# One attention and two expert layers on one core: a PSUM bank for every fourth block of the first layer, lows on another engine, and three small products put further back

## The chip, the cores and the metric

The program runs on one core of one Trainium2 chip. The metric is the device time of one execution in microseconds (us). Three executions of the kernel before took 758.89, 758.95 and 762.05 us; the median is 758.95 us. A fourth execution was recorded by the hardware profiler.

The engines are named as in the profile: PE is TensorE (PEld its weight loads), DVE is VectorE, ACT is ScalarE, POOL is GpSimd, SP is SyncE, which here only issues DMAs. Each engine runs its own instructions in their order, and waits for others by semaphores.

## The reference

Three stages, each the input of the next (4 x 768 = 3072 tokens, 384 columns):

```python
# attention, per batch and head; f = sigmoid(f_logit)
state = f[:, :, t, :, None] * state + einsum('bhd,bhe->bhde', k[:, :, t], v[:, :, t])
y[:, :, t] = einsum('bhd,bhde->bhe', q[:, :, t], state)
# first layer: 384 -> 2048 -> 384
h = x @ w_in;  x = np.maximum(0.01 * h, h) @ w_out
# second layer: 8 experts (384 -> 1024 -> 384), 384 tokens each
logits = x @ w_gate
# all (token, expert) pairs in falling order of their logit: a token goes to the first expert that has room
for e in range(E):
    out[assigned == e] = np.maximum(x[assigned == e] @ w1[e], 0.0) @ w2[e]
```

## The kernel before

**Numbers.** PE multiplies 16-bit numbers. Where more accuracy is wanted, a value is kept as a 16-bit high part and a 16-bit rest, its low part, and a product is made of three: high by high, high by low, low by high. A 128 x 384 block of the first layer's hidden values (tile `hp`, one PSUM bank) is so the sum of nine matmuls of 384 columns.

**First layer.** The 24 attention tiles of 128 tokens form eight groups of three, `gi` = 0 to 7. `first(gi)` makes the 16 blocks `f` of a group's hidden values: nine matmuls into `hp`, then ACT copies it scaled by 0.01, DVE takes the larger of the two (both tile `g`, in SBUF), and for each pair of blocks ACT makes the high part `gh` and DVE the low part `gl`. A bank of `hp` is free when DVE's `g` has read it. `second(gi, n, m)` multiplies `gh` and `gl` by `w_out` into `xp`, three times per group. The order is first(0), first(1), second(0), first(2), second(1), and so on to first(6); first(7) has the router's `logits` of the groups 5 and 6 among its blocks (tile `lp`), and the second halves of the groups 5, 6 and 7 come after it.

**PSUM.** There are eight banks. The pool `psum` has three of them under the tag `mm`, which `hp` and `xp` (later also the experts' `hp` and `yp`) take in turn. The pool `banks[0]` has five under the tag `at`, which the attention's products take in turn: `P`, two `A`, `kT`, `y`, `U` for a tile, and the early gate products `pg`. For first(7) that pool is closed and another, `banks2`, takes its five banks: three for the router (tag `rt`, `lp` among them) and two for turned tokens.

**What sets the order.** A driver runs first and second as the main stream and attention, the weights' preparation and later the router and the token lists as side streams: each yields the number of nanoseconds of main-stream matmuls after which it is taken up again. The tile framework's scheduler then orders each engine's instructions by its own estimates, save those given to `keep_in_program_order`. Beside the first layer, ACT and DVE also split the experts' weights (`xw_s` is loaded, ACT makes `xw_h`, DVE `xw_l`, SP stores both).

**Second layer.** `route()` finds in seven rounds which tokens each expert gets. A round has levels of three small products with DVE between them (`ge` by `oh` into `c`, then `cnt`, then `tot`) and ends in `slots_of`, which counts places by two products with `ones` and `tri` into `ps`. `token_list` turns places into a list of token numbers by the products `pi` (with `ohs` and `rh`) and `pj`; POOL then fetches the tokens by indirect DMAs (`xg`), SP turns them by DMA (`x2T`). `expert(r)` makes eight `hp` blocks of nine matmuls, ACT writes the high part `hh`; the low part `hl` is made by DVE for odd `f`, and for even `f` of experts 0 to 5 by POOL from a second copy that ACT writes (tile `g` in the profile). Then three `yp` of 24 matmuls each go out through POOL's scatter. The seventh round's lists are those of experts 6 and 7 (`E - 2` and `E - 1`).

Every instruction shows as line 85, the recording helper, so the profile is read by tile names.

Of the kernel before, what the change touches and what calls it, by code (L numbers as in the profile page):

```python
# [9 lines left out]
F32 = mybir.dt.float32  # L10
# [82 lines left out]
def body(tc, qk, v, f_logit, w_in, w_out, w_gate, w1, w2, out):  # L93
# [8 lines left out]
    E = w_gate.shape[1]  # L102
# [4 lines left out]
    GW = 384  # L107
# [5 lines left out]
    with ExitStack() as ctx:  # L113
# [4 lines left out]
        psum = ctx.enter_context(tc.tile_pool(name="psum", bufs=1, space=bass.MemoryType.PSUM))  # L118
        ctxL, ctxR, ctxP = (ctx.enter_context(ExitStack()) for _ in range(3))
        banks = [ctxP.enter_context(tc.tile_pool(name="banks", bufs=1, space=bass.MemoryType.PSUM, reuse_waits="tile"))]  # L120
# [9 lines left out]
        def mm(o, l, r, start, stop):  # L130
            return PE.matmul(o, l, r, start=start, stop=stop, skip_group_check=True)
# [405 lines left out]
        def first(gi, nn, gx):  # L537
            xh, xl = gx[:, :KT], gx[:, KT:]
            N = 128 * nn
            gp = g2pool[0] if gi == LAST else gpool  # L540
            gh = gp.tile([128, NF, GW], F16, name="gh")
            gl = gp.tile([128, NF, GW], F16, name="gl")
            gh_[gi], gl_[gi] = gh, gl
            for f in range(NF):
                while ("in", f * NPC // NF) not in ready:
                    yield None
                fs = slice(128 * f, 128 * (f + 1))
                hp = psum.tile([128, GW], F32, name="hp", tag="mm", bufs=3)[:, :N]
                for c in range(KT):
                    mm(hp, winh[:, c, fs], xh[:, c, :N], c == 0, False)  # L550
                    yield N / 2.4
                    mm(hp, winh[:, c, fs], xl[:, c, :N], False, False)
                    yield N / 2.4
                    mm(hp, winl[:, c, fs], xh[:, c, :N], False, c == KT - 1)
                    if c < KT - 1:
                        yield N / 2.4
                a = SG / (SX * SWI)
                with tc.high_priority():
                    if f % 2 == 0:
                        g = work.tile([128, 2, GW], F32, name="g32")  # L560
                    t = g[:, f % 2, :N]
                    i = copy(t, hp, 0.01 * a)
                    fed.append((i, DVE.scalar_tensor_tensor(t, hp, a, t, op0=OP.mult, op1=OP.max)))
                    big[0] += 3 * KT
                    if f % 2:
                        s = slice(f - 1, f + 1)
                        copy(gh[:, s, :N], g[:, :, :N])
                if f % 2 == 0 and f:
                    tc.keep_in_program_order(low())
                if f % 2:  # L570
                    def low(s=s, g=g):
                        return DVE.tensor_tensor(gl[:, s, :N], g[:, :, :N], gh[:, s, :N], op=OP.subtract)
                yield N / 2.4
            low()
# [50 lines left out]
        R = {}  # L625
# [92 lines left out]
        def route():  # L718
# [6 lines left out]
            for rnd in range(E - 1):  # L725
# [73 lines left out]
                x48 = small([128, 2, NT], "x48", BF16)  # L799
# [16 lines left out]
                s1 = slots_of(x48, 2)  # L816
# [17 lines left out]
            x48 = small([128, 2, NT], "x48", BF16)  # L834
            for i in range(2):
                DVE.tensor_scalar(x48[:, i, :], asg, last[i], None, op0=OP.is_equal)
            yield 500.0
            s1 = slots_of(x48, 2)
            DVE.tensor_scalar(s1[:, 1, :], s1[:, 1, :], -float(NT * 128 // E), 0.0, op0=OP.add, op1=OP.max)
            for i in range(2):  # L840
                lists.append((E - 2 + i, s1[:, i, :]))
# [7 lines left out]
        GAP = (1700.0, 700.0, 550.0, 2000.0, 3400.0)  # L849
        lists = []  # L850

        def slots_of(x, n):

            w = n * NT
            xf = x.rearrange("p a b -> p (a b)")
            ps = bank([128, 2, 2 * NT], "ps")
            mm(ps[:, 1, :w], R["ones"], xf[:, :w], True, True)
            mm(ps[:, 0, :w], R["tri"], xf[:, :w], True, True)
            tot = small([128, 2 * NT], "totc")
            DVE.tensor_copy(tot[:, :w], ps[:, 1, :w])  # L860
            inc = small([128, 2 * NT], "inc")
            DVE.tensor_tensor_scan(inc[:, :w], R["ones"][:, :w], tot[:, :w], 1.0, op0=OP.mult, op1=OP.add)
            DVE.tensor_tensor(inc[:, :w], inc[:, :w], tot[:, :w], op=OP.subtract)
            s = small([128, 2, NT], "s1")
            sf = s.rearrange("p a b -> p (a b)")
            DVE.tensor_tensor(sf[:, :w], ps[:, 0, :w], inc[:, :w], op=OP.add)
            DVE.tensor_tensor(sf[:, :w], sf[:, :w], xf[:, :w], op=OP.mult)
            return s

        def token_list(r, s):  # L870

            si = small([128, NT], "si", I32)
            DVE.tensor_scalar(si, s, -1.0, None, op0=OP.add)
            lo = small([128, NT], "lo", I32)
            DVE.tensor_scalar(lo, si, 31, None, op0=OP.bitwise_and)
            hi = small([128, NT], "hi", I32)
            DVE.tensor_scalar(hi, si, 5, None, op0=OP.arith_shift_right)
            lob = small([128, NT], "lob", BF16)
            DVE.tensor_scalar(lob, lo, 1.0, None, op0=OP.add)
            hib = small([128, NT], "hib", BF16)  # L880
            DVE.tensor_copy(hib, hi)
            yield 2500.0 if r else 600.0

            G = 4
            one = rw.tile([128, NT // G, 32, G], BF16, name="ohs", bufs=1)
            for h in range(2):
                x = slice(NT // G // 2 * h, NT // G // 2 * (h + 1))
                lg4 = lob.rearrange("p (a g) -> p a g", g=G)[:, x, None, :].to_broadcast([128, NT // G // 2, 32, G])
                DVE.tensor_tensor(one[:, x], lg4, R["thr5"][:, x], op=OP.is_equal)
                yield 300.0  # L890
            h12 = small([128, 12, NT], "h12", BF16)
            DVE.tensor_tensor(h12, hib[:, None, :].to_broadcast([128, 12, NT]), R["i12"], op=OP.is_equal)
            rh = small([128, 2, 12, NT], "rh", BF16)
            DVE.tensor_tensor(rh[:, 0], h12, R["jn"], op=OP.mult)
            DVE.tensor_scalar(rh[:, 1], h12, pcol, None, op0=OP.mult)
            yield 1800.0
            pi = bank([128, 24, G], "pi")
            for a in range(NT // G):
                mm(pi, one[:, a], rh[:, :, :, a * G:(a + 1) * G].rearrange("p v h g -> p (v h) g"),
                   a == 0, a == NT // G - 1)  # L900
            pm = small([128, 24, G], "pm", F16)
            DVE.tensor_tensor(pm, pi, R["d15"][:, None, :].to_broadcast([128, 24, G]), op=OP.mult)
            pd = small([128, 24], "pd", F16)
            with nc.allow_low_precision("one whole number and zeros"):
                DVE.tensor_reduce(pd, pm, axis=AX.X, op=OP.add)
            yield 1200.0
            pj = bank([128, 6, 4], "pj")
            mm(pj, R["join"], pd, True, True)
            pq = small([128, 6, 4], "pq")
            DVE.tensor_tensor(pq, pj, R["quarter"][:, None, :].to_broadcast([128, 6, 4]), op=OP.mult)  # L910
            ti = small([128, 2, 3], "ti")
            DVE.tensor_reduce(ti.rearrange("p a b -> p (a b)"), pq, axis=AX.X, op=OP.add)
            idx = rw.tile([128, 3], I32, name="idx", bufs=E)
            DVE.scalar_tensor_tensor(idx, ti[:, 0, :], 128.0, ti[:, 1, :], op0=OP.mult, op1=OP.add)

            row = rw.tile([128, 3], I32, name="row", bufs=E)
            if r:
                DVE.tensor_scalar(row, idx, 1.0, None, op0=OP.add)
            else:
                f = small([128, 3], "f3")  # L920
                DVE.tensor_scalar(f, idx, 1.0, None, op0=OP.add)
                DVE.scalar_tensor_tensor(row, f, float(NT * 128 - 128), f, op0=OP.is_le, op1=OP.mult)
                DVE.tensor_scalar(R["place"], R["i384"], s[:, NT - 1:NT], None, op0=OP.is_equal)
            LISTS["x", r] = row, idx
# [69 lines left out]
        def expert(r):  # L994
# [20 lines left out]
            for f in range(NF1):  # L1015
# [8 lines left out]
                        yield N / 2.4  # L1024
                with tc.high_priority():
                    ACT.activation(hh[:, f, :], hp, AF.Relu, bias=0.0, scale=1.0)
                    if f % 2 == 0 and r < E - 2:
                        t = work.tile([128, 2 * GW], F32, name="g32")[:, :N]
                        ACT.activation(t, hp, AF.Relu, bias=0.0, scale=1.0)
                        POOL.tensor_tensor(hl[:, f, :], t, hh[:, f, :], op=OP.subtract)  # L1030
                    else:
                        DVE.scalar_tensor_tensor(hl[:, f, :], hp, 0.0, hh[:, f, :], op0=OP.max, op1=OP.subtract)
# [295 lines left out]
```

## Time and profile before

| | us |
|---|---|
| median of the three runs | 758.95 |
| the profiled execution | 760.42 |
| its span, first to last instruction | 758.6 |
| PE busy with matmuls | 722.8 |
| DVE busy | 548.5 |
| ACT busy | 339.8 |
| POOL busy | 94.4 |

The span and the engines' busy times are of the profiled execution; 1.8 us of its 760.42 lie outside the span. Busy times overlap. A matmul of 384 columns is recorded as 0.33 us long while the next one starts 0.16 us after it, so time that PE loses is read from start to start.

### The profile page before, as it was taken

To read this page: it belongs to the slowest core of one execution; us is meant where nothing else is said; L and a number is where in the kernel's file an instruction comes from. 1 tells how busy PE (TensorE), PEld (TensorE's weight loads), DVE (VectorE), ACT (ScalarE), POOL (GpSimd) and SP (SyncE) were. 2 spreads that over 40 slices of the span, in tenths; PEclk is the share of its full clock that TensorE was granted. 3 is DMA by queue.
4 is the path that set the end of the run, shared out by engine and by line. 5 is a ranking of instruction groups with operands and counts; after the bars stand their busy time and mean duration, and the time that the engine had idled before them with its cause. 6 is when DMAs were issued, how large, how long until landed. Compare 5 with 4: busy or idle time off the path is not lost.

```text
span 758.6 us, 15366 instructions
## 1 busy us (share of the span) xinstructions
PE 722.8 (95%) x5871; PEld 472.8 (62%) x5871; DVE 548.5 (72%) x1607; ACT 339.8 (45%) x708; POOL 94.4 (12%) x124
## 2 busy tenths in 40 slices
PE   8997899999999999999999999999999999999995
PEld 6774666677676577566666666555555555556663
DVE  7999999998857867876964858687686776873220
ACT  7677555567736755754753652000123123222220
POOL 3000000000000000000000001010244534535111
PEclk9999999999999999999999999999999999999998
DMA  9997554799896898998899300050396566677500
GB/s 230 208 251 200 156 143 133 198 294 253 232 268 180 238 262 203 265 272 223 218 269 244 131 2 2 23 197 22 109 266 168 167 196 159 230 193 212 149 31 32
DMA packets 116444, 137.09 MB, mean 181 GB/s; under 512 B 67729, under 2 KB 99474, under 8 KB 114322
## 3 DMA queue, kind: packets, MB, share of 16 engines
q1 hardware_dynamic: 110994, 101.50, 52.0%
q0 software_dynamic: 5376, 34.61, 13.5%
q8 instruction: 46, 0.75, 0.4%
q14 instruction: 28, 0.23, 0.1%
HBM read 86.52 MB, written 34.60 MB: 160 GB/s over the span
## 4 chain that ended last, share of the span: by engine, by line
PE 50%; DVE 21%; DMA 11%; issue 10%; ACT 3%; POOL 3%; SPq 1%; POOLq 0%; ACTq 0%; DVEq 0%
PE hp L85 19%; PE xp L85 17%; PE yp L85 4%; DMA fT<-in_f_logit 4%; PE y L85 3%; DVE g L85 3%; DVE woutu L85 2%; DVE gl L85 2%; DMA xw_s<-in_moe_w 2%; DMA win_e<-in_moe_w_in 1%; PE A L85 1%; PE c L85 1%; PE P L85 1%; POOL out L85 1%; DVE am L85 1%
## 5 line engine op out<-in xcount | busy, mean ns | idle before, releaser
L85 PE MATMUL hp<-xT,winh 128*128 128x384 f16 x768 | 190.7, 328 | 10.0 <-ACT winh L85 4.9
L85 PE MATMUL xp<-wo,gh 128*128 128x384 f16 x768 | 191.1, 326 | 2.8 <-DVE g L85 1.8
L85 PE MATMUL hp<-xT,winl 128*128 128x384 f16 x384 | 125.6, 328 | 0.5 <-DVE winl L85 0.4
L85 PE MATMUL xp<-wo,gl 128*128 128x384 f16 x384 | 125.0, 326 | 0.0
L85 PEld LDWEIGHTS <-gh 128*128 128x128 f16 x912 | 83.9, 97 | 45.7 <-issue 3.2
L85 PEld LDWEIGHTS <-winh 128*128 128x128 f16 x768 | 73.2, 98 | 53.8 <-issue 7.2
L85 PE MATMUL hp<-x2T,w1e 128*128 128x384 f16 x576 | 98.9, 326 | 0.4 <-ACT x2T L85 0.3
L85 PE MATMUL yp<-w2e,hh 128*128 128x384 f16 x384 | 94.4, 326 | 0.0
L85 DVE SCALAR_TENSOR_TENSOR g<-hp,g 128x384 f32<-128x384 f32 x128 | 70.2, 554 | 28.1 <-ACT g L85 27.7
L85 ACT ACTIVATE g<-hp 128x384 f32<-128x384 f32 x152 | 72.0, 484 | 37.1 <-PE hp L85 26.5
L85 PEld LDWEIGHTS <-w1e 128*128 128x128 f16 x576 | 52.4, 97 | 32.8 <-issue 0.7
L85 ACT ACTIVATE gh<-g 128x768 f16<-128x768 f32 x64 | 53.9, 842 | 29.0 <-DVE g L85 28.9
L85 PEld LDWEIGHTS <-gl 128*128 128x128 f16 x528 | 48.9, 97 | 28.5 <-DVE gl L85 0.5
L85 ACT ACTIVATE xw_h<-xw_s 128x768 f16<-128x768 f32 x64 | 53.1, 839 | 29.0 <-DMA xw_s<-in_moe_w 23.9
L85 PE MATMUL yp<-w2e,hl 128*128 128x384 f16 x192 | 62.5, 326 | 0.0
L85 DVE TENSOR_TENSOR gl<-g,gh 128x768 f16<-128x768 f32 x64 | 60.9, 952 | 2.0 <-ACT gh L85 2.0
L85 DVE SCALAR_TENSOR_TENSOR xw_l<-xw_s,xw_h 128x768 f16<-128x768 f32 x64 | 60.2, 951 | 1.7 <-ACT xw_h L85 1.5
L85 ACT ACTIVATE hh<-hp 128x384 f16<-128x384 f32 x64 | 31.4, 490 | 59.7 <-PE hp L85 53.7
L85 POOL IOTA jp<- 128x128 f32 x2 | 0.5, 237 | 455.8 <-PE hp L85 455.7
L85 ACT ACTIVATE x<-yp 128x384 f32<-128x384 f32 x24 | 11.8, 490 | 91.1 <-PE yp L85 76.4
L85 PEld LDWEIGHTS <-winl 128*128 128x128 f16 x384 | 37.6, 98 | 24.0 <-DVE winl L85 1.7
L85 DVE SCALAR_TENSOR_TENSOR hl<-hp,hh 128x384 f16<-128x384 f32 x40 | 22.2, 555 | 41.2 <-ACT hh L85 41.0
(262 smaller groups left out, 1123.9 us busy)
## 6 DMA issues: line engine op xcount, KB each, us to landing
xw_s<-in_moe_w SPq DMA_DIRECT2D x64, 384.0 KB, 4.2
qkT<-in_qk SPq DMA_DIRECT2D x48, 192.0 KB, 5.1
wout_s<-in_moe_w_out SPq DMA_DIRECT2D x16, 384.0 KB, 3.3
w1d<-xw_h SPq DMA_DIRECT2D x32, 192.0 KB, 4.1
w1d<-xw_l SPq DMA_DIRECT2D x32, 192.0 KB, 4.2
w2d<-xw_h SPq DMA_DIRECT2D x32, 192.0 KB, 3.6
w2d<-xw_l SPq DMA_DIRECT2D x32, 192.0 KB, 4.4
fT<-in_f_logit SPq DMA_DIRECT2D x24, 192.0 KB, 3.9
```

The costliest lines, as they stand in the source:

```text
L85: i = f(*args, **kwargs)
```

## The change

Four edits. In `first`, the blocks `f` = 3, 7, 11 and 15 of the groups 2 to 6 take their bank from the attention's five instead of `mm`'s three. In `expert`, the low parts of even blocks of expert 0 are made by DVE, as odd ones are, and no longer by ACT and POOL. After the last round, the stream yields 3100 instead of 500 before the last `slots_of`, and the first of its two products is kept in program order. For expert 6, `token_list` yields 1500 instead of 1800 before `pi`.

```diff
@@ first
-                hp = psum.tile([128, GW], F32, name="hp", tag="mm", bufs=3)[:, :N]
+                if f % 4 == 3 and 2 <= gi < LAST:
+                    hp = banks[0].tile([128, GW], F32, name="hp", tag="at", bufs=5)[:, :N]
+                else:
+                    hp = psum.tile([128, GW], F32, name="hp", tag="mm", bufs=3)[:, :N]
@@ route, after the last round
-            yield 500.0
-            s1 = slots_of(x48, 2)
+            yield 3100.0
+            s1 = slots_of(x48, 2, tc.keep_in_program_order)
@@ slots_of
-        def slots_of(x, n):
+        def slots_of(x, n, put=lambda i: None):
...
-            mm(ps[:, 1, :w], R["ones"], xf[:, :w], True, True)
+            put(mm(ps[:, 1, :w], R["ones"], xf[:, :w], True, True))
@@ token_list
-            yield 1800.0
+            yield 1500.0 if r == E - 2 else 1800.0
@@ expert
-                    if f % 2 == 0 and r < E - 2:
+                    if f % 2 == 0 and 0 < r < E - 2:
```

What the scheduler makes of it is more than the diff tells. On PE, the order up to the last group is the same, and only the banks differ. At the start of first(7), where `hp` is that group's first block and `lp` are the router's logits, the order before was:

```order
L85 LDWEIGHTS winh
L85 MATMUL hp<-xT,winh 128x384
L85 LDWEIGHTS gh
L85 MATMUL lp<-wgc,gh 128x16
L85 LDWEIGHTS gl
L85 MATMUL lp<-wgc,gl 128x8
L85 LDWEIGHTS winh
L85 MATMUL hp<-xT,winh 128x384
```

and now is (rows from the block's eighth matmul on):

```order
L85 LDWEIGHTS winh
L85 MATMUL hp<-xT,winh 128x384
L85 LDWEIGHTS winl
L85 MATMUL hp<-xT,winl 128x384
L85 LDWEIGHTS gh
L85 MATMUL lp<-wgc,gh 128x16
L85 LDWEIGHTS gl
L85 MATMUL lp<-wgc,gl 128x8
L85 LDWEIGHTS gh
L85 MATMUL lp<-wgc,gh 128x16
```

The logits begin behind all nine matmuls of the block instead of behind its first, and the first 18 of them follow each other. The second logits tile takes the bank that the last block of group 6 had.

On DVE, in expert 0, between the first round's slots and the next round's `ge` (which PE's product `c` waits for; `key`, `di` and `v` are steps of the router, `hl` the low parts), the order was:

```order
L85 TENSOR_TENSOR eq_7646<-lg,m 128x192
L85 SCALAR_TENSOR_TENSOR hl<-hp,hh 128x384
L85 TENSOR_TENSOR s_7632<-ps,inc 128x48
L85 TENSOR_SCALAR key<-m 128x24
L85 TENSOR_TENSOR eq_7646<-eq_7646,wdt 128x192
L85 TENSOR_TENSOR s_7632<-s_7632,x_7594 128x48
```

and now is:

```order
L85 TENSOR_SCALAR wi<-mx,p_6230 128x1
L85 SCALAR_TENSOR_TENSOR hl<-hp,hh 128x384
L85 SCALAR_TENSOR_TENSOR inc<-ones,totc 128x48
L85 TENSOR_REDUCE m<-lg 128x24
L85 TENSOR_TENSOR inc<-inc,totc 128x48
L85 TENSOR_TENSOR eq_7640<-lg,m 128x192
L85 TENSOR_TENSOR s_7626<-ps,inc 128x48
L85 TENSOR_SCALAR key<-m 128x24
L85 TENSOR_TENSOR eq_7640<-eq_7640,wdt 128x192
L85 SCALAR_TENSOR_TENSOR hl<-hp,hh 128x384
L85 TENSOR_TENSOR s_7626<-s_7626,x_7590 128x48
```

All eight low parts of expert 0 now stand in DVE's order ahead of that `ge`; four did before. From the last level of round 0 (its `tot`) to the `ge` there are five instead of three. On PE the product `c` behind this `ge` stands six matmuls of 384 columns later than before. In expert 5, the last `ps` stands four such matmuls later, and `pi` and `pj` of experts 6 and 7 stand 14 later.

On POOL, while expert 5 runs (`hl` its low parts, `xg` the tokens of expert 6, `w1e` the weights of expert 7), the order was:

```order
L85 DMA out<-x_9653,idx 3072x384
L85 TENSOR_TENSOR hl<-g_9718,hh 128x384
L85 DMA xg<-x2d,row 128x768 x3
L85 TENSOR_TENSOR hl<-g_9774,hh 128x384
L85 TENSOR_TENSOR hl<-g_9819,hh 128x384
L85 DMA w1e<-w1d,wi 128x6144
```

and now is:

```order
L85 DMA out<-x_9623,idx 3072x384
L85 TENSOR_TENSOR hl<-g_9699,hh 128x384
L85 DMA xg<-x2d,row 128x768
L85 TENSOR_TENSOR hl<-g_9766,hh 128x384
L85 DMA xg<-x2d,row 128x768 x2
L85 TENSOR_TENSOR hl<-g_9795,hh 128x384
L85 DMA w1e<-w1d,wi 128x6144
```

One low part now stands between the first and the second fetch.

## Rows read from the trace of the kernel before

**Rows 1.** The page, part 1: busy time, share of the span, instructions

```profile
PE 722.8 (95%) x5871; PEld 472.8 (62%) x5871; DVE 548.5 (72%) x1607; ACT 339.8 (45%) x708; POOL 94.4 (12%) x124
```

**Rows 2.** Waits of PE, 180 to 470: us in total, times, longest us

```profile
PE hp L85 <- DVE g L85: 3.2, 5, 1.6
PE xp L85 <- DVE g L85: 1.8, 1, 1.8
```

**Rows 3.** Waits of PE, 230 to 260, in first(4)

```profile
PE hp L85 <- DVE g L85: 2.6, 3, 1.6
```

**Rows 4.** Timeline of PE, first(4): start, length, instruction, [idle before <-releaser]

```profile
248.68 0.49 PE L85 MATMUL hp<-xT,winh 128*128 128x384 f16 x2 [1.62 <-DVE g L85]
...
251.60 0.49 PE L85 MATMUL hp<-xT,winh 128*128 128x384 f16 x2
```

**Rows 5.** Timeline of ACT, first(4)

```profile
246.81 0.84 ACT L85 ACTIVATE xw_h<-xw_s 128x768 f16<-128x768 f32 x1 [2.02 <-DMA xw_s<-in_moe_w]
```

**Rows 6.** Timeline of DVE, first(4)

```profile
248.06 0.56 DVE L85 SCALAR_TENSOR_TENSOR g<-hp,g 128x384 f32<-128x384 f32 x1 [1.82 <-ACT g L85]
...
249.40 0.55 DVE L85 SCALAR_TENSOR_TENSOR g<-hp,g 128x384 f32<-128x384 f32 x1
```

**Rows 7.** Timeline of ACT behind the wait of `xp`

```profile
197.03 0.84 ACT L85 ACTIVATE xw_h<-xw_s 128x768 f16<-128x768 f32 x1 [0.97 <-DMA xw_s<-in_moe_w]
197.78 0.58 ACT L85 ACTIVATE kp<-kT 128x512 f32<-128x512 f32 x1
```

**Rows 8.** Timeline of PE there

```profile
199.06 0.95 PE L85 MATMUL U<-ld_v,kp 128*112 128x96 f32 x8
```

**Rows 9.** Timeline of PE, the first matmul of first(7)

```profile
433.90 0.33 PE L85 MATMUL hp<-xT,winh 128*128 128x384 f16 x1
```

**Rows 10.** Timeline of DVE, the last block of group 6

```profile
435.79 0.55 DVE L85 SCALAR_TENSOR_TENSOR g<-hp,g 128x384 f32<-128x384 f32 x1
```

**Rows 11.** Timeline of PE, expert 0

```profile
561.22 0.33 PE L85 MATMUL yp<-w2e,hl 128*128 128x384 f16 x1
563.30 0.32 PE L85 MATMUL c<-oh,ge 128*128 128x32 bf16 x6 [1.75 <-DVE ge L85]
```

**Rows 12.** Timeline of DVE, expert 0

```profile
557.60 0.55 DVE L85 SCALAR_TENSOR_TENSOR hl<-hp,hh 128x384 f16<-128x384 f32 x1
558.06 0.19 DVE L85 TENSOR_TENSOR s<-ps,inc 128x48 f32<-128x48 f32 x1
558.18 0.92 DVE L85 TENSOR_SCALAR key<-m 128x24 int32<-128x24 int32 x1
...
559.18 0.91 DVE L85 TENSOR_TENSOR s<-s,x 128x48 f32<-128x48 f32 x1
...
562.70 0.55 DVE L85 TENSOR_TENSOR ge<-v,thr 128x768 bf16<-128x768 bf16 x1
```

**Rows 13.** Timeline of POOL, expert 0

```profile
558.13 1.90 POOL L85 TENSOR_TENSOR hl<-g,hh 128x384 f16<-128x384 f32 x2
```

**Rows 14.** Timeline of PE, expert 5

```profile
678.22 0.18 PE L85 MATMUL ps<-x,ones 128*128 128x48 bf16 x1 [0.52 <-DVE x L85]
...
682.88 0.42 PE L85 MATMUL pi<-rh,ohs 128*128 128x96 bf16 x6 [1.20 <-DVE rh L85]
```

**Rows 15.** Timeline of DVE, expert 5

```profile
682.44 0.39 DVE L85 TENSOR_SCALAR rh<-h,pcol 128x288 bf16<-128x288 bf16 x1
```

**Rows 16.** Timeline of POOL, expert 5: the weights of expert 7

```profile
692.45 0.96 POOL L85 DMA_INDIRECT w1e<-w1d,wi  x1
```

**Rows 17.** Timeline of SP, expert 5: the third turn of expert 6's tokens

```profile
692.37 1.21 SPq L85 DMA_TRANSPOSE x2T<-xg  x1
```

**Rows 18.** DMA issues from 560.5 to 560.8: median us to landing

```profile
w1e<-w1d,wi POOLq DMA_INDIRECT x1, 7.5
x2T<-xg SPq DMA_TRANSPOSE x1, 7.8
```

**Rows 19.** Timeline of PE, the start of expert 6

```profile
703.43 0.98 PE L85 MATMUL hp<-x2T,w1e 128*128 128x384 f16 x5
```

## The prediction

> **The bound.** I read the page first: PE is busy for 722.8 of 758.6 us [rows 1], so the time is the length of PE's own queue plus its waits, and a change that moves no matmul can only gain what PE waits. Then the waits of PE. In the first layer from 180 us on, nearly all are of one kind: `hp`, five times, 3.2 us, and `xp`, once, 1.8 us, both for DVE's `g` [rows 2]. That is a bank still being read. With three banks, a block must wait for the `g` of the third block ahead of it. These numbers are a little short, since idle time is counted from the recorded end of a matmul, 0.33 us long, where the next could start after 0.16 (two blocks of nine take 251.60 - 248.68 = 2.92 us, so 0.162 a matmul [rows 4]). Six waits at 0.16 more each make 5.0 + 1.0 = 6.0 us lost.
>
> The timelines show whose fault it is. The longest, ahead of the block at 248.68, ends with the `g` of 248.06 [rows 4, 6]; that one waited 1.82 us for ACT, and ACT had stood 2.02 us in front of a weight split whose load had not landed [rows 5]. So DVE and ACT fall behind for reasons of their own, and PE's few banks pass it on.
>
> In the second layer, I looked for PE's longest single waits that lie where the change acts: `c` for `ge` in expert 0, 563.30 - 561.22 - 0.16 = 1.9 us [rows 11], and in expert 5 `ps`, 0.52 + 0.16 = 0.7, and `pi`, 1.20 + 0.16 = 1.4 us [rows 14].
>
> **Banks.** 2.2 us gained, between 0 and 6.0. Of four blocks, three now take `mm`'s banks, so a block there waits for the `g` of the fourth block ahead of it; the fourth takes one of the attention's five. PE's lead over DVE grows by one block, 9 x 0.162 = 1.46 us. Upper end: all 6.0 us. Lower end: nothing, if ACT, DVE and the DMAs stay where they are and later waits take it all back. Two places show how much is kept at once.
>
> The `xp` that waited has its bank free long before, so 1.96 us go. But soon after it, `U` needs `kp`, which ACT makes at 197.78 to 198.36 behind a split that waited for a load [rows 7]; nothing of that is moved by PE. `U` started at 199.06 [rows 8] and can now start at 198.4: 0.7 us is kept.
>
> In first(4), three waits up to 248.68 cost 2.6 us as shown [rows 3], so 3.1 with 0.16 added to each. After it DVE works without a pause, and its `g` of 249.40 ends at 249.95 [rows 6]: the block at 251.60 is four behind that one, so it cannot start before 250.0. 1.6 us is kept of 3.1, about the one block of lead.
>
> In first(5) the last two go, 3.2 - 2.6 + 0.3 = 0.9 us [rows 2, 3], but there PE, ACT and DVE wait for each other and for loads in turn, and I count nothing. That makes 0.7 + 1.6 = 2.3; I take 2.2, nearer the low end. For the rest to pass on to the end, everything behind must start earlier too. Attention, `x`, `turned` and the weight loads are issued when PE or DVE has freed a tile, so they move with it.
>
> **Attention's banks.** Nothing, with one exception. 20 blocks now hold an attention bank. By the times of the trace each finds its bank free well before, since an attention bank comes round only after five. What covers it is that distance; the price, if it is too short, is the rival below.
>
> **Logits.** At first(7) 0.9 us lost, between 0 and 1.5. This is the exception. The second `lp` tile takes the bank of group 6's last block, whose `g` is read from 435.79 to 436.34 [rows 10]. The last group's first block, which now runs whole ahead of the logits, starts at 433.90 [rows 9] and takes 1.46 us, so PE stands from about 435.4 to 436.4. The low end is that `g` moves up into DVE's free time, the high end that PE's greater lead meets it earlier.
>
> **Lows.** In expert 0 1.5 us gained, between 0 and 1.9. ACT loses four copies and POOL four subtractions; both have idle time there, so this alone is worth nothing. DVE gets four lows, at 558.06 - 557.60 = 0.46 us each [rows 12]. But while POOL ran its two lows at 558.13 [rows 13], two tiny DVE steps took 0.92 and 0.91 us where one of the same size took 0.19 [rows 12]: 0.73 + 0.72 = 1.45 us lost. In the stretch that ends in `ge`, which DVE works through without a pause, two lows come in (0.92) and 1.45 go: `ge` ends at 562.70 + 0.55 - 0.53 = 562.7. The product `c` stands six matmuls later, and PE would be there at 561.22 + 7 x 0.163 = 562.36. It waits 0.4 instead of 1.9 us. If the slow steps stay, `ge` ends at 564.2 and nothing is gained.
>
> **Last lists.** 1.6 us gained, between 0.4 and 2.0. `ps` stands four matmuls later, 0.65 us, which is its wait of 0.7. It then starts where it did, 678.22 [rows 14], so DVE's chain behind it keeps its times, save that one low (0.46) now stands ahead of `rh`: `rh` ends at 682.83 + 0.46 = 683.3 [rows 15]. `pi` stands 14 later than before, 30 behind `ps`: 678.3 + 30 x 0.163 = 683.2. It waits about 0.15 instead of 1.4. Together 2.05 - 0.25 = 1.8.
>
> What is late next: the tokens of expert 6. The list comes about when it did, but on POOL a low of 0.9 us now stands between the fetches, so the third turn comes some 0.6 us later. In the trace it was issued at 692.37, just ahead of the weights of expert 7 at 692.45 [rows 16, 17]; now it falls behind them. Where a turn was issued with such weights under way it took 7.8 us, landing as they did (7.5) [rows 18]. So it lands near 693.0 + 7.8 = 700.8, and expert 6, which began at 703.43 [rows 19], would want it at 703.43 - 1.8 = 701.6. That is close; I take off 0.2, and up to 1.4 for the low end.
>
> The Trainium skill, "DMA: Bandwidth & Descriptors", section "Queues, rings and completion order", says that a DMA engine takes turns packet by packet between the queues that have work. By that rule SP's turn would not be held by POOL's weights, the 0.2 would be 0, and the sum 4.6 instead of 4.4; the 7.8 beside 7.5 in the trace speaks for the longer time.
>
> The list of expert 7 comes later by 14 matmuls, 2.3 us; the whole of expert 6, 144 matmuls at 0.162 or 23 us, lies between it and its use: nothing.
>
> **The sum.** 2.2 - 0.9 + 1.5 + 1.6 = 4.4 us. The profiled execution took 760.42 us, 758.6 of it the span; it would take 756.0. The median of the runs is 1.5 us under it, 758.95, so I predict 754.6. A difference of 0.5%, 3.8 us, is about what a measurement can tell from no change.
>
> **Rivals.** First, the first layer gives it all back. The lead of one block is lost again where PE waits for something that does not move: `kp`, or for a turned tile of the gate's early products. Against it: those DMAs are issued behind PE's own work. -0.9 + 1.5 + 1.6 = 2.2 gained: 756.8.
>
> Second, all bank waits go, and ACT and DVE keep up. For it: DVE has idle time between the episodes. Against it: the block at 251.60. 6.0 - 0.9 + 1.5 + 1.6 = 8.2 gained: 750.7.
>
> Third, slower: the attention runs short of banks. A block holds its bank for its nine matmuls and until DVE's `g`, and DVE is sometimes two blocks late. If an attention product, say `A` or `y`, then stands in PE's queue in front of a bank not yet read, PE stops for all. One wait as long as the longest of the trace, 1.8 us [rows 2], in each of the five groups is 9.0, and the gain of 2.2 is gone: 9.0 + 0.9 - 1.5 - 1.6 = 6.8 lost, 765.8. It decides from 6.0 us on (3.8 + 2.2), 0.3 for each of the 20 blocks. Against it: the distance of five.
>
> **The numbers.** My case has 0.55, and two thirds of it lie under 755.16: 0.37 faster, 0.18 same. The first rival has 0.25, all of it same; the second 0.15, faster; the third 0.05, slower. So faster 0.52, same 0.43, slower 0.05. The range goes from the second rival, 750.6, to the first with its other terms near their low ends (0.9 and 0.9, so 0.9 gained), 758.2.
>
> **To look for.** Right: no wait of `hp` for `g` over 0.3 us from 180 to 330; one new wait of `lp` for DVE near 434; `c` in expert 0 waiting under 0.8 us and no DVE step of 128x24 near 0.9 us there; `ps` and `pi` in expert 5 under 0.4 us; first(7) starting 1 to 3 us earlier. Wrong: waits of `A`, `kT`, `y` or `U` for `g`; first(7) starting when it did; expert 6 waiting for `x2T` by more than a microsecond.

## The result and the profile after

The changed kernel took 774.78 us (median of six executions) where the kernel before took 758.43 (six, the three shown ahead among them): ratio 1.013, 95% interval 1.0085 to 1.0175. That is slower by about 10 us, where 4.4 faster was forecast, and it lies outside the range. The six times are 763.75, 764.25, 774.57, 774.98, 776.94 and 779.05. Ratios, here and below, leave out executions over 1.5% above the fastest of their kernel (here 776.94 and 779.05), so this one says 10 us where the medians are 16 apart. The profiled execution took 774.57, with a span of 772.8.

The page, part 1, of the kernel after, answers [rows 1]; PE's busy time has grown by 3.4 us, although PE has the same 5871 matmuls:

```profile
PE 726.2 (94%) x5871; PEld 474.4 (61%) x5871; DVE 548.0 (71%) x1611; ACT 338.1 (44%) x704; POOL 90.7 (12%) x120
```

The waits of PE from 650 us on (what waits, for what: us in total, times, longest) hold the whole loss in a line. Before, the waits there were those of [rows 14], and none was for `x2T`:

```profile
PE hp L85 <- DMA x2T<-xg: 16.8, 1, 16.8
PE pj L85 <- DVE pd L85: 0.2, 1, 0.2
```

The timeline of PE around it: expert 5's last product, then expert 6's first ([rows 19] before).

```profile
697.58 0.33 PE L85 MATMUL yp<-w2e,hl 128*128 128x384 f16 x1
714.66 0.80 PE L85 MATMUL hp<-x2T,w1e 128*128 128x384 f16 x2 [16.76 <-DMA x2T<-xg]
```

Expert 6 could have begun at 697.74, 5.7 us before the old 703.43, and began 11.2 us after it. What released it is the turn of its tokens. The rest of the loss stands in the windows of the kernel after (stretch, length, busy time of PE, PEld, DVE, ACT and POOL with counts, granted clock, DMA share, GB/s):

```profile
697.00:714.60 17.60, 0.90 (x6) 0.32 (x4) 0.00 (x0) 0.49 (x1) 1.95 (x2) 0.68 1.12 254
714.70:720.00 5.30, 5.30 (x17) 2.50 (x18) 0.56 (x1) 0.49 (x1) 0.00 (x0) 0.50 0.29 61
720.00:730.00 10.00, 10.00 (x62) 5.95 (x61) 3.46 (x7) 3.43 (x7) 0.00 (x0) 0.98 0.00 0
```

PE had stood for 17 us, and then ran for 5.3 us at a granted clock of 0.50, that is at 1.2 instead of 2.4 GHz: half of 5.3, 2.7 us more. That is about the 2.9 us that the part from expert 6 on is longer (last row of the table).

Here is the whole span by stages, from first matmul to first matmul as the timelines of PE give them (us):

| stage | before | after | difference |
|---|---|---|---|
| start to first(1) | 82.24 | 80.91 | -1.33, nothing changed there |
| first(1) to first(7), 82.24 to 433.90 | 351.66 | 349.02 | -2.64 |
| first(7) to expert 0 | 113.27 | 114.35 | +1.08 |
| expert 0 | 27.66 | 26.39 | -1.27 |
| experts 1 to 4 | 102.55 | 102.57 | +0.02 |
| expert 5 up to the start of expert 6 | 26.05 | 41.42 | +15.37 |
| from there to the end | 55.19 | 58.11 | +2.92 |

So the three gains and the one loss of the forecast are there (expert 5 without its wait, 41.42 - 16.92 = 24.50, is 1.55 shorter than before), and one stage, whose loss had been put at 0.2 us, took back far more than all the gains.

**How the tokens came late.** The timeline of POOL, kernel after (before: fetches at 686.48, 687.76 and 689.03, weights as in [rows 16]):

```profile
682.68 0.99 POOL L85 DMA_INDIRECT xg<-x2d,row  x1 [2.67 <-DVE row L85]
683.70 0.92 POOL L85 TENSOR_TENSOR hl<-g,hh 128x384 f16<-128x384 f32 x1
684.78 0.98 POOL L85 DMA_INDIRECT xg<-x2d,row  x1 [0.16 <-issue]
686.07 0.95 POOL L85 DMA_INDIRECT xg<-x2d,row  x1 [0.30 <-issue]
687.03 0.92 POOL L85 TENSOR_TENSOR hl<-g,hh 128x384 f16<-128x384 f32 x1
688.11 0.96 POOL L85 DMA_INDIRECT w1e<-w1d,wi  x1 [0.16 <-PE pj L85]
689.37 0.94 POOL L85 DMA_INDIRECT xg<-x2d,row  x1 [0.30 <-DVE row L85]
690.91 0.99 POOL L85 DMA_INDIRECT out<-x,idx  x1 [0.59 <-ACT x L85]
```

The third turn on SP's queue, kernel after (before: [rows 17]):

```profile
690.67 1.84 SPq L85 DMA_TRANSPOSE x2T<-xg  x1
```

And the DMA issues (op, count, median us to landing): before, the third turn (692.3 to 692.6) and the weights; then, kernel after, the second turn (688.05 to 688.2), the third (690.6 to 690.7) and the weights:

```profile
x2T<-xg SPq DMA_TRANSPOSE x1, 5.6
w1e<-w1d,wi POOLq DMA_INDIRECT x1, 8.7
...
x2T<-xg SPq DMA_TRANSPOSE x1, 16.0
...
x2T<-xg SPq DMA_TRANSPOSE x1, 23.9
...
w1e<-w1d,wi POOLq DMA_INDIRECT x1, 14.5
```

Counted from the first fetch, the third turn is issued 7.99 us later, where it was 5.89 before; the weights come 5.43 us after that fetch instead of 5.97. Before, the turn went out 0.08 us ahead of the weights and took 5.6 us. Now it goes out 2.56 us behind them and takes 23.9, and the weights themselves take 14.5 where they had taken 8.7. In between stands expert 7's first token fetch, at 689.37, ahead of the output. The second turn is caught as well: issued at 688.07, 0.04 us ahead of the weights, it takes 16.0 us, where that of the kernel before (690.84) took 3.2, and the third is behind it on SP's queue.

### The profile page after: what moved, and what is told of

The parts are those of the page before. It is cut to its first block, busy times and chain, and to the rows that moved or that the text cites. A ratio compares the mean times of both kernels' runs of the same rounds, so it can differ in the third digit from the quotient of the medians.

```text
span 772.8 us, 15362 instructions
## 1 busy us (share of the span) xinstructions
PE 726.2 (94%) x5871; PEld 474.4 (61%) x5871; DVE 548.0 (71%) x1611; ACT 338.1 (44%) x704; POOL 90.7 (12%) x120
## 3 DMA queue, kind: packets, MB, share of 16 engines
q0 software_dynamic: 5376, 34.61, 14.5%
## 4 chain that ended last, share of the span: by engine, by line
PE 44%; DVE 26%; DMA 12%; issue 11%; ACT 5%; SPq 1%; POOL 1%; POOLq 0%; ACTq 0%; DVEq 0%
PE xp L85 15%; PE hp L85 13%; PE yp L85 5%; DVE g L85 4%; DMA xw_s<-in_moe_w 3%; DVE gl L85 3%; DMA fT<-in_f_logit 3%; PE y L85 3%; DVE xw_l L85 2%; DVE woutu L85 2%; DMA w1e<-w1d,wi 2%; PE P L85 2%; PE A L85 1%; PE U L85 1%; PE c L85 1%
## 5 line engine op out<-in xcount | busy, mean ns | idle before, releaser
L85 PE MATMUL hp<-x2T,w1e 128*128 128x384 f16 x576 | 101.6, 332 | 17.1 <-DMA x2T<-xg 16.8
L85 ACT ACTIVATE g<-hp 128x384 f32<-128x384 f32 x148 | 70.0, 484 | 37.2 <-PE hp L85 26.3
L85 DVE SCALAR_TENSOR_TENSOR hl<-hp,hh 128x384 f16<-128x384 f32 x44 | 24.4, 555 | 60.3 <-ACT hh L85 60.1
```

Source lines behind the costliest of these rows:

```text
L85: i = f(*args, **kwargs)
```

## The experiments

Four theories were put against each other. **Theory 1**: the list edits (the third and fourth) let the third turn of expert 6's tokens meet expert 7's weights on the DMA queues, and that holds it. **Theory 2**: it is the low part between the fetches on GpSimd that makes the turn late. **Theory 3**: the earlier edits have a part in the loss, as they bring PE to expert 6 earlier. **Theory 4**: it is expert 7's first token fetch, which now stands between the weights and the third turn. The edits are numbered as in the change. Each kernel is compared with the kernel before on the same chip, where that took 765.18 us (first four kernels), 764.41 (second four) and 764.77 (last four) in the median.

### One edit, or some of them

The first edit alone:

```diff
+                if f % 4 == 3 and 2 <= gi < LAST:
+                    hp = banks[0].tile([128, GW], F32, name="hp", tag="at", bufs=5)[:, :N]
```

> The first edit alone (every fourth block of the first layer, groups 2 to 6, in an attention bank). Theory 1, the list edits alone lose the time (expert 6's token turns and expert 7's weight load hold each other): 0.5 to 2.5 us faster than before, my terms being 2.2 gained and 0.9 lost, and expert 6 waits for its turned tokens by under 1 us. Theory 3, the earlier edits have a part in the loss because PE reaches expert 6 earlier: slower than before, and expert 6 waits for x2T by several us.

Ratio 0.9978 (0.9955 to 1.0001), 1.7 us faster with an interval that touches no change. No wait for `x2T`.

The second edit alone:

```diff
-                    if f % 2 == 0 and r < E - 2:
+                    if f % 2 == 0 and 0 < r < E - 2:
```

> The second edit alone (low parts of expert 0's even blocks by VectorE). Theory 1: 1.0 to 1.9 us faster than before, c in expert 0 waits 0.4 us instead of 1.75, and expert 6 waits for x2T by under 1 us. Theory 3: slower than before, with a wait for x2T.

0.9962 (0.9937 to 0.9987), 2.9 us faster, more than the 1.0 to 1.9 expected though the interval reaches down to 1.0, and no wait for `x2T`.

Both of these, without the list edits:

> The first and second edit, without the two on the lists. Theory 1: 2.0 to 4.0 us faster than before (2.2 - 0.9 + 1.5 = 2.8), no wait of expert 6 for x2T over 1 us. Theory 3: as slow as the changed kernel, 6 to 16 us over before, with that wait.

0.9942 (0.9917 to 0.9967): 4.4 us faster, a little over the 2.0 to 4.0 expected and about the sum of the two.

The third and fourth edit alone:

```diff
-            yield 500.0
-            s1 = slots_of(x48, 2)
+            yield 3100.0
+            s1 = slots_of(x48, 2, tc.keep_in_program_order)
...
-            yield 1800.0
+            yield 1500.0 if r == E - 2 else 1800.0
```

> The third and fourth edit alone (3100 for 500 before the last slots, the ones product in program order, 1500 for 1800 before expert 6's pi). Theory 1: slower than before by 4 to 18 us, expert 6 waits 5 to 17 us for x2T, and expert 7's weights, issued between or just after the turns, take over 12 us to land instead of 8.7. Theory 3: faster than before by 1 to 2 us, without that wait.

1.0083 (1.0047 to 1.0119), 6.4 us slower. The profile is of one of its three longest executions (785.41; the other six took 769.2 to 775.9). The wait of PE, and the issue of the third turn (703.12, 2.42 us behind the weights), in it:

```profile
PE hp L85 <- DMA x2T<-xg: 16.4, 1, 16.4
...
x2T<-xg SPq DMA_TRANSPOSE x1, 23.7
```

Theory 3 falls: the two earlier edits gain alone and together, and the list edits lose without them.

Edits one, two and four, without the third:

> Edits one, two and four, without the third (500 stays before the last slots). The fetches of expert 6 stand together and two low parts before expert 7's fetch and weights, as in the kernel before save that expert 7's first token fetch stands ahead of the weights. Theories 1 and 2: the turns are ahead of the weights, no wait over 1 us, 2 to 4 us faster than before. A rival, that any change of the lists' order costs: expert 6 waits 5 us or more.

0.9924 (0.9894 to 0.9954), 5.8 us faster where 2 to 4 were expected, no wait for `x2T`; `ps` and `pi` wait as before. It is the third edit that does the harm. In this kernel, expert 7's first token fetch stands even ahead of the weights, at 691.52, but the third turn is out by then, at 691.02.

### What holds the turn

All four edits, but the weights of expert 7 are asked for only when expert 6's tokens are turned: their row numbers pass through a GpSimd step that reads all three turns.

```diff
+            if r == E - 1:
+                wi = small([128, NM], "wj", I32, E)
+                last_x = LISTS["t", E - 2][:, 0, 127::128]
+                POOL.tensor_scalar(wi, last_x, 0.0, LISTS["wf", r], op0=OP.mult, op1=OP.add)
...
```

> All four edits, but the row numbers of expert 7's weights pass through a GpSimd step that reads all three turned tiles of expert 6, so the weights are asked for only when the tokens are turned; expert 7's first token fetch then stands behind the next output. Theory 1 (weights asked for while turns are under way make turns and weights hold each other): the turns land within 8 us of their issue, expert 6 waits for x2T by under 1 us, 3 to 5 us faster than before. Theory 4 (expert 7's first token fetch, between the weights and the third turn, does it): the same here, it tells nothing. A rival to both, that the later list alone is too late whatever the DMAs do: expert 6 still waits 3 us or more, and no gain.

0.9968 (0.9947 to 0.9989), 2.4 us faster. The wait for `x2T` is gone, the third turn takes 2.8 us, and the rival falls: the list is not too late by itself. Expert 5 takes 24.50 us, 1.5 less than before. That the gain is under the 3 to 5 expected has two visible parts: in expert 6 `hp` waits once for DVE's `hl` (0.8 + 0.16), and it takes 24.39 us where it takes 23.40 in the kernels that wait for nothing there; in expert 4 `tot` waits 0.3 us for DVE's `ok`, and it takes 25.57 instead of 25.02. What causes these two waits stays open.

All four edits, with expert 7's list later, so that its token fetches come behind the output:

```diff
-            yield 1200.0
+            yield 4000.0 if r == E - 1 else 1200.0
             pj = bank([128, 6, 4], "pj")
```

> All four edits, but expert 7's list yields 4000 instead of 1200 before pj, so that on GpSimd the next output and then the three token fetches follow expert 7's weights; expert 6's fetches, turns and the weights keep the changed kernel's order. Theory 1: no help, expert 6 waits 5 to 17 us for x2T, 4 to 17 us slower than before. Theory 4: the wait falls under 2 us, and it is 2 to 4 us faster than before.

0.9989 (0.9962 to 1.0015), and two of its twelve executions took 775.55 and 775.75 beside 761.4 to 766.8 of the others. The wait of expert 6 and the third turn's landing (issued 697.46, 2.17 us behind the weights):

```profile
PE hp L85 <- DMA x2T<-xg: 3.0, 1, 3.0
...
x2T<-xg SPq DMA_TRANSPOSE x1, 10.5
```

Neither theory came out as written. Without the fetch in between, the turn still takes 10.5 us instead of 5.6, so the weights hold it (theory 1). The price is lower than with the fetch, but beside a profile of about the same length (12.2 us, the changed kernel again, below) only by 1.7 us; a part of theory 4's fetch isn't excluded, and isn't shown.

All four edits, and the one low part that stood between the fetches by VectorE:

```diff
-                    if f % 2 == 0 and 0 < r < E - 2:
+                    if f % 2 == 0 and 0 < r < E - 2 and (r, f) != (E - 3, 4):
```

> All four edits, but one low part of expert 5 (block 4) by VectorE instead of GpSimd, so that expert 6's three token fetches follow each other without a low part between them; then a low part, expert 7's weights and its first token fetch, as in the changed kernel. Theory 2 (the low part between the fetches makes the third turn late): turns issued 1.3 us apart and ahead of the weights, expert 6 waits under 1 us, 3 to 5 us faster than before. Theory 1: the same if the third turn is issued ahead of the weights; if it is issued behind them, a wait of 5 to 17 us stays. Theory 4: the wait goes only if the turn is issued ahead of expert 7's token fetch.

0.9944 (0.9919 to 0.9969), 4.3 us faster. The turn was not ahead of the weights, as theory 2 had it, but 1.25 us behind them (693.88 and 692.63), and ahead of expert 7's fetch (694.42):

```profile
PE hp L85 <- DMA x2T<-xg: 0.4, 1, 0.4
...
x2T<-xg SPq DMA_TRANSPOSE x1, 9.6
```

Of what was expected, theory 4's came out: the turn is ahead of the fetch, and the wait is gone. Theory 1's wait of 5 to 17 us behind the weights did not come; the turn is held here too, 9.6 us, but lands just in time. The low part did not matter by its own 0.9 us: the weights follow the third fetch by 2.05 us here (690.58 and 692.63) as by 2.04 in the changed kernel. But the third fetch takes 3.3 us to its turn, where it takes 4.2 to 4.6 in the kernels with the low part between.

### The changed kernel again, smaller packets, and a version that beats both

The changed kernel as it is:

> The changed kernel as it is, once more, beside the versions below on the same chip. Theory 1 with what the trace of the changed kernel shows of the DMA queues (a 256-byte packet of a turn goes through per 12288-byte packet of the weights, and in some executions fifteen of the sixteen DMA engines stand for 6 us more): two groups of times, one 4 to 7 us over before and one 15 to 20 us over it. Theory 4 alone: the same.

1.0041 (0.9999 to 1.0084). The twelve times run from 763.8 to 783.1, six up to 768.7 and six from 773.9. So there are two groups, but lower than expected: -1.0 to 3.9 us over before, and 9.1 to 18.4. The profile is of 764.46 us, one of the shorter ones, and it has the same wait, for a turn issued at 692.75, 2.24 us behind the weights:

```profile
PE hp L85 <- DMA x2T<-xg: 4.8, 1, 4.8
...
x2T<-xg SPq DMA_TRANSPOSE x1, 12.2
```

So the mechanism is in the short executions too, at 4.8 us, and the long ones take some 10 more (medians 767.0 and 777.1).

Here the DMA queues show what the turn waits for. From 694 to 697 us, in this kernel (packets and MB, then by queue with the share of 16 engines; `q0` is POOL's, `q1` carries the turns):

```profile
DMA packets 110, 1.11 MB, mean 369 GB/s; under 512 B 20, under 2 KB 20, under 8 KB 20
...
q0 software_dynamic: 90, 1.11, 105.6%
q1 hardware_dynamic: 20, 0.00, 0.4%
```

The third turn is issued, and practically nothing of it passes (from 695 to 697 no packet of `q1` at all); the 90 packets are weights of 12288 bytes. In the changed kernel's first profile, from 706 to 708, packets of a turn and of weights (`w2e`) alternate instead, 60 and 60:

```profile
q0 software_dynamic: 60, 0.74, 86.9%
q1 hardware_dynamic: 60, 0.02, 3.4%
```

And from 691.8 to 697 it shows something else, which goes with the long wait. The DMA engines carry next to nothing:

```profile
DMA packets 51, 0.09 MB, mean 18 GB/s; under 512 B 40, under 2 KB 40, under 8 KB 46
```

Fifteen packets of weights, begun from 690.76 to 691.71, all end at 697.2, 5.5 to 6.5 us long, while single packets go through, at first one of the weights and one of a turn by turns, no two at a time. Some 50 of them are a turn's, about the 48 that are one engine's share of a turn's 768 (an estimate). Then it is the other way round: a lone packet of 4608 bytes takes 6.0 us, from 697.25 to 703.2, while weights go through fifteen at a time. The profile of the list edits alone has the same pair, fifteen of 6.1 to 6.8 us and then one of 6.2. In the short execution no packet there lasted over 2.2 us, and the second turn's packets of 256 bytes were through by 693.0, just as the weights' began.

All four edits, with those weights in four pieces:

```diff
+                if r == E - 1 and t is t1:
+                    n = t.shape[-1] // 4
+                    for a in range(4):
+                        POOL.indirect_dma_start(out=t[:, n * a:n * (a + 1)], out_offset=None,
+                                                in_=src.rearrange("r (k c) -> (r k) c", k=4),
...
```

> All four edits, but expert 7's first weights are fetched in four indirect DMAs of 3072 bytes a row instead of one of 12288; the third turn still follows the start of that load, and expert 7's first token fetch stands behind all four. Theory 1 with the packet sizes as the mechanism: a turn packet waits for 3072 bytes instead of 12288, the third turn lands in 4 to 8 us instead of 10 to 24, expert 6 waits under 1.5 us for x2T, 2 to 5 us faster than before and no group of long times. If not the size of the packets but any weight load under way holds the turn: 10 us or more for the turn and a wait of 3 us or more.

0.9952 (0.9925 to 0.9978), 3.7 us faster, with the third turn 2.16 us behind the first piece; the longest of its twelve executions took 766.74. The wait:

```profile
PE hp L85 <- DMA x2T<-xg: 1.1, 1, 1.1
```

Expert 6 began at 704.51, so the turn, issued at 695.82, took at most 8.7 us; 4 to 8 were expected. The packets were recorded with 6144 bytes, not 3072. Smaller pieces shorten the hold, as theory 1 says; since they also put expert 7's fetch behind the third turn and spread the load over four issues, the size alone isn't shown.

All four edits, the low part of block 4 by VectorE, and the weights behind the turns (the edits of two kernels above):

> All four edits, one low part of expert 5 (block 4) by VectorE, and expert 7's weights asked for through the GpSimd step that reads expert 6's turned tokens: no low part between the fetches and no weights under way while the turns run. Theory 1: turns land in 3 to 4 us each, no wait of expert 6 for x2T over 0.5 us, ps and pi do not wait, 4 to 6 us faster than before, and 0 to 1.5 us faster than the version without the third edit. A rival, that the list edits bring nothing once the DMAs are out of the way: 0.5 us or more slower than the version without the third edit.

0.9916 (0.9886 to 0.9946), 6.4 us faster, the fastest version tried: 758.4 us beside 764.77. Its waits of PE from 650 us on, with none for `x2T`, `ps` or `pi`:

```profile
PE hp L85 <- DVE hl L85: 0.4, 1, 0.4
PE tot L85 <- DVE ok L85: 0.3, 1, 0.3
PE pj L85 <- DVE pd L85: 0.2, 1, 0.2
```

Its three turns (issues from 687 to 694), the GpSimd step that waits for them, and the weights:

```profile
x2T<-xg SPq DMA_TRANSPOSE x3, 3.2
...
693.96 0.27 POOL L85 TENSOR_SCALAR wj<-x2T,wf 128x3 int32<-128x3 f16 x1 [4.42 <-DMA x2T<-xg]
694.68 1.01 POOL L85 DMA_INDIRECT w1e<-w1d,wj  x1 [0.45 <-POOL wj L85]
```

The version without the third edit, beside it:

> The version without the third edit once more (edits one, two and four), beside the others on the same chip: 2.5 to 5.5 us faster than before, no wait for x2T.

0.9939 (0.9911 to 0.9968), 4.7 us faster. The means of the two are 758.7 and 760.6, 1.9 apart with a standard error of 0.7, a difference that no stage of the profiles shows whole: expert 5 takes 24.49 us against 26.04, but the version above gives back 0.54 in expert 4 (`tot` waits for `ok`) and 0.58 in expert 6 (`hp` waits for `hl`). Experts 4 to 6 together are 0.4 shorter, so the profiles show little that the third edit adds.

Put together, by how long the third turn was issued behind the start of the weights (us; minus is ahead), with the lengths of experts 5 and 6 from the timelines of PE:

| kernel | behind | turn took | PE waits | expert 5 | expert 6 |
|---|---|---|---|---|---|
| all edits, block 4 and weights held | -3.68 | 2.8 | 0 | 24.49 | 23.98 |
| all edits, weights held | -3.72 | 2.8 | 0 | 24.50 | 24.39 |
| before | -0.08 | 5.6 | 0 | 26.05 | 23.40 |
| all edits, block 4 by VectorE | 1.25 | 9.6 | 0.4 | 25.10 | 23.39 |
| all edits, weights in four pieces | 2.16 | at most 8.7 | 1.1 | 25.73 | 23.40 |
| all edits, expert 7's list later | 2.17 | 10.5 | 3.0 | 27.65 | 25.06 |
| the change, again | 2.24 | 12.2 | 4.8 | 29.45 | 25.66 |
| list edits alone | 2.42 | 23.7 | 16.4 | 41.08 | 24.90 |
| the change | 2.56 | 23.9 | 16.8 | 41.42 | 26.20 |

The distance sorts the short waits. It does not explain the step from 12.2 to 23.7 us between 2.24 and 2.42: the last two rows are profiles with the standstill, the row above them is one without. Nor does it explain the changed kernel's second turn, 16.0 us at 0.04 ahead, beside 5.6 at 0.08.

## Why the prediction was wrong, by its steps

**The bound** was read rightly. The end is set by PE's queue and its waits, and the waits that the change aimed at gave way.

**Banks**, 2.2 gained between 0 and 6.0: right, 2.64 from first(1) to first(7). Over all profiles, that stretch is 347.1 to 349.5 us in the eleven with this edit and 350.1 to 352.8 in the three without. The waits of PE from 180 to 470 in the kernel after, beside [rows 2]:

```profile
PE U L85 <- ACT kp L85: 1.6, 2, 1.1
PE lp L85 <- DVE g L85: 0.9, 1, 0.9
PE hp L85 <- DVE g L85: 0.8, 1, 0.8
```

`xp` no longer waits, and `U` waits for `kp` in its place, as worked out. Of the five waits of `hp` one is left, ahead of the block that stood at 251.60 before ([rows 4]); "to look for" allowed it 0.3 us and it has 0.8, at the bank that the prediction named as four behind. By the count of PE's matmuls this block is in first(3), and the waits that were put in first(4) and first(5) lie in first(3) and first(4), which changes no number. The rival of the attention's banks did not come: no `A`, `kT`, `y` or `U` waits for `g`.

```profile
248.49 0.48 PE L85 MATMUL hp<-xT,winh 128*128 128x384 f16 x2 [0.81 <-DVE g L85]
...
432.53 0.17 PE L85 MATMUL lp<-wgc,gh 128*128 128x16 f16 x1 [0.94 <-DVE g L85]
```

**Logits**, 0.9 lost: right. The second row is the new wait, 0.94 by the profile; the stage lost 1.08.

**Lows**, 1.5 gained: right in kind, 1.27 in expert 0. The timeline of DVE there, with all lows on it ([rows 12] before):

```profile
554.35 0.56 DVE L85 SCALAR_TENSOR_TENSOR hl<-hp,hh 128x384 f16<-128x384 f32 x1
...
555.74 0.17 DVE L85 TENSOR_SCALAR key<-m 128x24 int32<-128x24 int32 x1
...
556.46 0.20 DVE L85 TENSOR_TENSOR s<-s,x 128x48 f32<-128x48 f32 x1
...
559.29 0.54 DVE L85 TENSOR_TENSOR ge<-v,thr 128x768 bf16<-128x768 bf16 x1
```

The two steps that took 0.92 and 0.91 us beside GpSimd's lows take 0.17 and 0.20. The timeline of PE, expert 0 ([rows 11] before) and then expert 5 ([rows 14]):

```profile
559.89 0.32 PE L85 MATMUL c<-oh,ge 128*128 128x32 bf16 x6 [0.26 <-DVE ge L85]
...
679.07 0.42 PE L85 MATMUL pi<-rh,ohs 128*128 128x96 bf16 x6
...
681.02 0.17 PE L85 MATMUL pj<-pd,join 128*128 128x24 f16 x1 [0.24 <-DVE pd L85]
```

`c` loses 0.26 + 0.16 = 0.42 us where 0.4 was worked out.

**Last lists**, 1.8 gained before what is late next: right in kind, 1.55. `ps` and `pi` wait no more, `pj` waits 0.24 + 0.16 = 0.4, and expert 5 is that much shorter wherever nothing holds the tokens (26.05 to 24.50).

**What is late next** is the step that failed. "I take off 0.2, and up to 1.4 for the low end": it cost 16.9 us in the first profile and 5.0 in the second (16.76 + 0.16 and 4.79 + 0.16), and then the clock. The place was right, to the third turn falling behind expert 7's weights, and it stood among the things that would show the prediction wrong. Three terms of it were mis-sized. With the turn's true time of issue but the old price, 690.67 + 7.8 = 698.5, PE would have waited 0.7 us: most of the loss is the price.

First, the turn is 2.1 us later against the first fetch, not 0.6. The low part moved the third fetch by 0.84, and that fetch then took 4.6 us to its turn (686.07 to 690.67), where it had taken 3.3 (689.03 to 692.37), beside a turn that was already running. The weights in turn come 0.54 us earlier against the first fetch, so that 0.08 us ahead became 2.56 behind (2.10 + 0.54).

Second, the price of a turn behind weights was taken from one place, 7.8 us beside 7.5 [rows 18], and read as "landing as they did". There the turn was issued 0.39 us behind the weights (560.57 and 560.18). The same trace held higher prices, beside loads of `w2e`: for a turn issued 2.02 us behind one (605.12 and 603.10) and for one 0.49 behind (629.72 and 629.23):

```profile
x2T<-xg SPq DMA_TRANSPOSE x1, 8.8
...
x2T<-xg SPq DMA_TRANSPOSE x1, 9.8
```

In the table, 1.25 us behind costs 9.6 and 2.2 us behind costs 10.5 to 12.2: the turn does not end with the weights, but begins when they are nearly through (in the short execution no packet of `q1` from 695 to 697, in a load of 692.7 to 698.3), and shares the engines with the output and the fetches that GpSimd has queued by then. That the weights do this is shown by the kernels that ask for them later, 2.8 us, together with the one that moves only expert 7's fetch away, 10.5. That the longest waits need more than weights is shown too; what makes fifteen engines stand for 6 us is not, and remains open. Without expert 7's fetch in between long executions were rarer, 2 of 12 against 6 of 12, which is too few to settle it.

Third, a wait on PE was priced by its length alone. The wait of 3.0 us and that of 4.8 were followed by stretches at a granted clock of about 0.5, as that of 16.8 was; expert 6 took 25.06 and 25.66 us instead of 23.40. After the wait of 0.4 us, and that of 1.1, it took 23.4. The windows behind the wait of 3.0 and then of 4.8 us (columns as above):

```profile
708.00:710.00 2.00, 1.92 (x7) 0.94 (x8) 0.00 (x0) 0.00 (x0) 0.00 (x0) 0.52 1.13 442
...
705.10:708.00 2.90, 2.90 (x10) 1.35 (x11) 0.00 (x0) 0.00 (x0) 0.00 (x0) 0.50 1.00 417
```

The Trainium skill's rule, "DMA: Bandwidth & Descriptors", section "Queues, rings and completion order", that a DMA engine takes turns between queues packet by packet, was weighed and read as "the turn is not held". The stretch from 706 to 708 agrees with the rule; that from 694 to 697, where the third turn is issued and gets no packet, does not show it, and whether any packet of it stood in the queue by then the trace doesn't tell. But where it holds, it gives the turn one packet of 256 bytes for each of 12288, 0.02 MB beside 0.74: taking turns by packet is no protection for the queue with the small ones. So the sum "4.6 instead of 4.4" did not follow from the rule.

**The rivals** asked whether the gain in the first layer would stand, and it did. The side "slower" got 0.05, all of it for the attention's banks. The mechanism that decided was in the text, with a price from one row and no chance of its own; with the ends of the table, known only now, it would have been the strongest rival. The upper end of the range is a slip of 0.15: 0.9 gained gives 758.05, not 758.2. It decides nothing here.

## What to carry to other kernels

Before moving a product that ends in a fetch, write down for each DMA what was issued just ahead of it, what just behind it, and by how much: here a transposing DMA that had left 0.08 us ahead of a load of 1.6 MB left 2.5 us behind it, and 1.5 us of gain became 16.9 of waiting. A price taken from one place holds for that distance only, so the low end should be as wide as the distance is new. Where a small urgent transfer and a big patient one meet, let the big one depend on the small one, or cut it up; both turned the same four edits from slower into faster. But weigh that against leaving the order alone: without the third edit the kernel was 4.7 and 5.8 us faster than before, and the fastest version with it 6.4.

## What was not expected of the hardware

- The DMA engines nearly stood, all at once: in 5.2 us, 691.8 to 697, the sixteen moved 0.09 MB, with fifteen packets of 12288 bytes open for 5.5 to 6.5 us, which took 0.46 to 0.48 each from 697.7 on. It came in two of the profiles, each time with a turn's packets and the weights in flight together.
- After a wait of 3.0 us PE ran at about half clock and lost 1.7 us more in expert 6; after one of 4.8 it lost 2.3, after those of 16.4 and 16.8 it lost 1.5 and 2.8. After waits of 0.4 and 1.1 it lost nothing.
- In the profiles of all twelve experiments, but neither in that of before nor in that of after, `cnt` waits for `cd` two to four times in experts 0 to 3, up to 2.2 us each, and in eleven of them DVE stands for up to 3.3 us for something that the trace only calls remote, as in this row of the kernel with the weights held. The changed kernel run again has it too, so no edit brings it. Its cause stays open, and no profile tells whether the kernel before, 6 to 7 us slower on these chips, has it there; because of it experts 0 to 3 are compared only between before and after.

```profile
569.93 0.19 DVE L85 TENSOR_TENSOR cm<-c,diag 128x32 f16<-128x32 f32 x1 [1.94 <-remote]
```
